# Constants of an attention-and-maxout kernel: two memsets split in halves, a third made a ScalarE copy

## The chip, the cores and the metric

The kernel runs on one core of a Trainium2 chip. A core has five engines that run their own instruction streams and meet at semaphores: TensorE (PE in the profile, its weight loads PEld), VectorE (DVE), ScalarE (ACT), GpSimd (POOL) and SyncE (SP). Data moves between device memory and the on-chip SBUF by DMA queues that SyncE, GpSimd and ScalarE issue; matmul results land in PSUM. The metric is device time in microseconds, the median over runs.

## What is computed

```python
def mab(q, kv):
    s = scale * (q @ kv.transpose(0, 2, 1))
    s = s - s.max(-1, keepdims=True)
    a = np.exp(s)
    a /= a.sum(-1, keepdims=True) + 1e-09
    return a @ kv
h = mab(I, x)                 # 32 inducing points attend to x: (4, 12544, 128)
attn = mab(x, h)              # every row of x attends to the 32 results
g = np.maximum(attn @ w1, attn @ w2)      # (50176, 1024)
out = g @ w_out                           # (50176, 128)
```

The input has four batches of 12,544 rows of 128, the two weight matrices are 128x1024 and the last is 1024x128.

## The kernel before

Everything lies in one function, `tile_isab_inducing__then__act_maxout2_kernel`. The order of the instructions on each engine is written out by hand (`tc.manual_schedule`): a small model of the engines' times, the class `Clock`, decides while the program is built which step comes next, and what results is a fixed list for each engine.

**The head.** SyncE loads the first 14 of 98 chunks of batch 0 as f32 (`xf`, L202) and the inducing points. GpSimd loads the other chunks and casts them to f16 on the way (`load_x`, L165). In between it makes two identity matrices (`make_identity`, which the profile lists under masks.py). After the loads of x come those of the weights (L211 to L213). Meanwhile VectorE sets constants:

- `warm`, 128x512 f16, zero (L214). Operand of nine matmuls (L694) that TensorE runs before any data is there, of fillers later (L794), and of one matmul in each pooling sum.
- `ones16` and `ones32`, 128x128 in f16 and f32, one (L215, L216). A column of `ones16` sums the exponentials of batch 0 (L284) and of the remainder of later batches. `ones32` has no other use.
- `ones_q`, 128x4 f16: zero (L217), then a one in column q for the 32 partitions of quarter q (L219). Operand of the matmul that sums each quarter's exponentials (L670).

Then VectorE and ScalarE cast the first chunks, `xf` to f16 (L690, L691); TensorE transposes them (L233); VectorE and ScalarE copy the results out of PSUM (L244, L247); scores, exponentials (L272) and sums over batch 0 follow, by the list of steps `HEAD`. This part ends at about 24 us.

**The main part.** For each block of 16 chunks (four quarters of up to four chunks, one quarter on 32 partitions each) TensorE makes the scores (L611), ScalarE their exponentials (L630), TensorE four matmuls at a time on its four row groups (`phase`, L1021); VectorE or ScalarE takes the relu of each result (L1037, L1040); TensorE multiplies by `woutp` (L837); VectorE scales the result by the reciprocal of the sum (L864); SyncE stores it. The maximum of w1 and w2 is computed as a relu of the difference plus a linear term. The next batch's pooling (L327, L338, L383) runs in between.

The constants are set in this piece of the head, on VectorE except for the last line:

```python
nc.vector.memset(warm, 0.0)
nc.vector.memset(ones16, 1.0)
nc.vector.memset(ones32, 1.0)
nc.vector.memset(ones_q, 0.0)
for q in range(4):
    nc.vector.memset(ones_q[32 * q : 32 * (q + 1), q : q + 1], 1.0)
nc.gpsimd.memset(m1bd, 0.0)
```

Of the kernel before, what the change touches and what calls it, by code (L numbers as in the profile page):

```python
# [102 lines left out]
def kernel(  # L103
# [9 lines left out]
    nc = tc.nc  # L113
# [64 lines left out]
    ones32 = consts.tile([128, 128], F32, name="ones32")  # L178
    ones16 = consts.tile([128, 128], F16, name="ones16")
    warm = consts.tile([128, 512], F16, name="warm")  # L180
    ones_q = consts.tile([128, 4], F16, name="ones_q")
# [15 lines left out]
    with tc.manual_schedule(engines={ET.PE, ET.DVE, ET.Activation, ET.Pool, ET.SP}):  # L197
# [13 lines left out]
            nc.gpsimd.dma_start(out=w1h[:, lo : lo + 512], in_=moe_w1[:, lo : lo + 512])  # L211
            nc.gpsimd.dma_start(out=w2h[:, lo : lo + 512], in_=moe_w2[:, lo : lo + 512])
        nc.gpsimd.dma_start(out=woutp, in_=moe_w_out.rearrange("(jb j) c -> j jb c", j=128))  # L213
        nc.vector.memset(warm, 0.0)  # L214
        nc.vector.memset(ones16, 1.0)  # L215
        nc.vector.memset(ones32, 1.0)  # L216
        nc.vector.memset(ones_q, 0.0)  # L217
        for q in range(4):
            nc.vector.memset(ones_q[32 * q : 32 * (q + 1), q : q + 1], 1.0)  # L219
        nc.gpsimd.memset(m1bd, 0.0)  # L220
# [1050 lines left out]
```

## Time and profile before

| | |
|---|---|
| median of 3 runs | 327.14 us (327.10 to 327.21) |
| the profiled execution's own time | 327.28 us |
| its span, first to last instruction | 325.4 us |
| TensorE busy | 318.4 us, 98% of the span |
| VectorE busy | 284.3 us, 87% |
| ScalarE busy | 279.7 us, 86% |
| mean granted clock of TensorE | 1.00 |
| TensorE busy in the first 25 us | 21.5 us |
| TensorE busy from 60 to 300 us | 239.6 us of 240 |

The profile is one execution. A line of its timeline gives the start and the duration in microseconds, the engine, the source line, the operation, the tile written and the tile read, and how many instructions are merged in it; in brackets stands how long the engine was idle before, and what ended that. The chain of work that ended last is followed back from the last instruction, at each step to what released it. Starts are counted from the first instruction.

### The profile page before, as it was taken

The page shows a single profiled execution, that of the slowest core. Times are in us where ns is not written, and L with a number is a line of the kernel's source. Part 1 is how long each engine was busy: PE and PEld are TensorE (multiplying, and loading weights), DVE is VectorE, ACT ScalarE, POOL GpSimd, SP SyncE. Part 2 cuts the span into 40 slices and gives each one's busy share as a digit, 9 for nine tenths or more (in the row PEclk, how much of TensorE's full clock was granted, in tenths as well). Part 3 has the DMA queues.
Part 4 walks back from the last instruction along what each step waited for, and adds up shares of the span by engine and source line. Part 5 has one row for each costly group of instructions (what it writes and reads, how often), then busy time and mean ns, then how long its engine had stood idle before and what let it go on. Part 6 is the DMA issues. An engine that isn't in the chain of part 4 may idle for free.

```text
span 325.4 us, 12582 instructions
## 1 busy us (share of the span) xinstructions
PE 318.4 (98%) x5406; PEld 242.4 (74%) x5406; DVE 284.3 (87%) x512; ACT 279.7 (86%) x557; POOL 26.4 (8%) x53
## 2 busy tenths in 40 slices
PE   7899999999999999999999999999999999999996
PEld 3786777777777777777777777777777777777786
DVE  2469989989989998998989999998989999999973
ACT  3559899999888999998988999989969999999961
POOL 7262030000040000000040000000000000000000
PEclk9999999999999999999999999999999999999999
DMA  7999999985189999993479999885312312132133
GB/s 203 208 199 213 275 232 212 194 219 156 76 164 242 227 230 204 178 176 133 130 151 243 208 249 219 175 174 134 116 66 99 115 66 99 74 125 99 68 129 115
DMA packets 71831, 53.65 MB, mean 165 GB/s; under 512 B 52288, under 2 KB 57312, under 8 KB 71776
## 3 DMA queue, kind: packets, MB, share of 16 engines
q1 hardware_dynamic: 65232, 38.57, 49.3%
q0 software_dynamic: 6400, 14.22, 22.6%
q8 instruction: 42, 0.69, 1.0%
q14 instruction: 13, 0.11, 0.1%
q10 hardware_dynamic: 144, 0.07, 0.1%
HBM read 28.33 MB, written 25.69 MB: 166 GB/s over the span
## 4 chain that ended last, share of the span: by engine, by line
PE 93%; DMA 3%; ACT 2%; POOL 1%; issue 0%; DVE 0%; POOLq 0%
PE ps L837 61%; PE ps L1021 22%; DMA xn<-in_x_dram 3%; PE ps L611 2%; PE ps L327 2%; PE ps L383 1%; PE ps L233 1%; PE ps L670 1%; PE ps L301 1%; ACT relu L1037 1%; ACT xT L247 1%; PE ps L256 0%; PE ps L428 0%; PE ps L504 0%; ACT e L630 0%
## 5 line engine op out<-in xcount | busy, mean ns | idle before, releaser
L1037 ACT ACTIVATE relu<-ps 128x512 f16<-128x512 f32 x461 | 244.7, 602 | 27.6 <-PE ps L1021 19.2
L1040 DVE TENSOR_SCALAR relu<-ps 128x512 f16<-128x512 f32 x323 | 206.8, 682 | 16.6 <-PE ps L1021 14.9
L837 PE MATMUL ps<-woutp,relu 128*128 128x128 f16 x3136 | 217.3, 220 | 0.0
L837 PEld LDWEIGHTS <-relu 128*128 128x128 f16 x3136 | 176.7, 98 | 39.6 <-issue 29.3
L1021 PE MATMUL ps<-e,hwd 32*128 32x512 f16 (+2 forms) x888 | 88.7, 358 | 0.3 <-ACT e L630 0.3
L864 DVE TENSOR_TENSOR o<-ps,rp 128x512 f32<-128x512 f32 (+3 forms) x108 | 68.4, 634 | 5.5 <-PE ps L837 3.4
L1021 PEld LDWEIGHTS <-hwd 32*128 32x128 f16 x888 | 24.9, 91 | 21.1 <-issue 1.0
L1021 PE MATMUL ps<-m,e 32*128 32x128 f16 x381 | 38.7, 217 | 0.0
L1021 PEld LDWEIGHTS <-e 32*128 32x128 f16 x381 | 21.2, 92 | 2.6
L165 POOL DMA_DIRECT2D xn<-in_x_dram x31 | 16.8, 554 | 5.6 <-DMA xn<-in_x_dram 2.6
L244 DVE COPY xT<-ps 128x896 f16<-128x896 f16 (+3 forms) x11 | 5.8, 533 | 8.6 <-PE ps L233 8.5
L338 ACT ACTIVATE eu<-ps 128x512 f16<-128x512 f32 x18 | 10.8, 616 | 0.0
L630 ACT ACTIVATE e<-ps 128x512 f16<-128x512 f32 (+2 forms) x21 | 10.5, 577 | 0.0
L164 POOL COPY pace<-hacc 128x1 f32<-128x1 f32 x2 | 0.4, 183 | 114.0 <-DVE hacc L416 114.0
L233 PE MATMUL ps<-identity,xn 128*128 128x128 f16 x98 | 8.1, 229 | 1.4 <-DMA xn<-in_x_dram 1.4
L611 PE MATMUL ps<-xT,hT 128*32 128x512 f16 (+3 forms) x114 | 8.5, 362 | 0.0
L247 ACT COPY xT<-ps 128x896 f16<-128x896 f16 (+3 forms) x8 | 4.9, 640 | 3.9 <-PE ps L233 3.9
L233 PEld LDWEIGHTS <-xn 128*128 128x128 f16 x98 | 6.0, 102 | 2.9 <-DMA xn<-in_x_dram 1.8
L327 PE MATMUL ps<-xT,inducingT 128*32 128x512 f16 x72 | 6.5, 385 | 0.0
L272 ACT ACTIVATE et<-ps 128x224 f16<-128x224 f32 (+3 forms) x11 | 4.1, 410 | 2.5 <-PE ps L256 1.7
L611 PEld LDWEIGHTS <-hT 128*32 128x32 f16 x114 | 3.2, 94 | 3.8 <-issue 2.5
L383 PE MATMUL ps<-xn,eT 128*32 128x128 f16 x288 | 5.5, 220 | 0.0
(92 smaller groups left out, 105.8 us busy)
## 6 DMA issues: line engine op xcount, KB each, us to landing
out_dram<-o SPq DMA_DIRECT2D x85, 256.0 KB, 2.4
xn<-in_x_dram POOLq DMA_DIRECT2D x24, 448.0 KB, 11.3
out_dram<-o SPq DMA_DIRECT2D x20, 128.0 KB, 1.9
xn<-in_x_dram POOLq DMA_DIRECT2D x5, 224.0 KB, 10.8
xn<-in_moe_w_dram POOLq DMA_DIRECT2D x4, 256.0 KB, 14.2
xT<-xn SPq DMA_TRANSPOSE x42, 3.9
xf<-in_x_dram SPq DMA_DIRECT2D x1, 512.0 KB, 3.6
xf<-in_x_dram SPq DMA_DIRECT2D x1, 384.0 KB, 4.1
```

What stands on the lines that cost most here:

```text
L165: nc.gpsimd.dma_start(out=xn_at[b, i][:, 0:n, :], in_=xr[b, :, k0 : k0 + n, :])
L233: nc.tensor.transpose(ps[:, j, :], xn_at[0, i][:, g + j, :], identity16)
L327: nc.tensor.matmul(out=ps[32 * g : 32 * (g + 1), :], lhsT=inducingT, rhs=xT_tiles[b % 2][:, U * u + 4 * g : U * u + 4 * (g + 1), :], start ...
L338: nc.scalar.activation(out=eu, in_=ps, func=AF.Exp, scale=scale, accum_out=st[b]["es"][:, u : u + 1])
L383: nc.tensor.matmul(out=ps[32 * g : 32 * (g + 1), 0:128], lhsT=eT[:, j, 32 * g : 32 * (g + 1)], rhs=xn_of(b, U * v + 4 * g + j), start=(j = ...
L611: nc.tensor.matmul(out=ps[32 * q : 32 * (q + 1), 128 * t : 128 * (t + n)], lhsT=hq, rhs=xT[:, c : c + n, :], start=True, stop=True, tile_p ...
L630: nc.scalar.activation(out=blk.e2[:, lo:hi], in_=ps[:, lo:hi], func=AF.Exp, scale=st[0]["rs"] if blk.b == 0 else scale,)
L837: nc.tensor.matmul(out=g.ps[:, 128 * c : 128 * (c + 1)], lhsT=g.blk.relu[q][:, 128 * (jb * w4 + t) : 128 * (jb * w4 + t + 1)], rhs=woutp[: ...
L864: nc.vector.tensor_mul(osb[:, 0:n, :], g.ps[:, 0 : n * C].rearrange("p (s c) -> p s c", s=n), rp)
L1021: nc.tensor.matmul(**seq[i])
L1037: nc.scalar.activation(out=dst, in_=src, func=AF.Relu)
L1040: nc.vector.tensor_scalar(out=dst, in0=src, scalar1=0.0, scalar2=None, op0=ALU.max)
```

## The change

Six lines replace four in the piece above. `warm` is set in two halves of 256 columns. `ones16` is no longer set by VectorE; ScalarE copies it from `ones32`. `ones_q` is cleared in two halves of 64 partitions. The order on VectorE becomes: warm, warm, ones32, ones_q, ones_q, then the four ones as before. It has one instruction more ahead of the cast of L690, and ScalarE has one more ahead of the cast of L691; its table load now stands before that copy. TensorE's first weight load waits for the first half of `warm`, its first matmul for the second. Nothing else differs in the instruction lists of the five engines but line numbers.

```diff
-        nc.vector.memset(warm, 0.0)
-        nc.vector.memset(ones16, 1.0)
+        nc.vector.memset(warm[:, 0:256], 0.0)
+        nc.vector.memset(warm[:, 256:512], 0.0)
         nc.vector.memset(ones32, 1.0)
-        nc.vector.memset(ones_q, 0.0)
+        nc.scalar.copy(out=ones16, in_=ones32)
+        for h in range(2):
+            nc.vector.memset(ones_q[64 * h : 64 * (h + 1), :], 0.0)
         for q in range(4):
             nc.vector.memset(ones_q[32 * q : 32 * (q + 1), q : q + 1], 1.0)
```

## The prediction

> **What bounds the kernel now.** I read the head of the profile's page first, then its chain of work that ended last, and then the timeline and that chain over the first microseconds, where every changed line lies.
>
> ```profile
> span 325.4 us, 12582 instructions
> PE 318.4 (98%) x5406; PEld 242.4 (74%) x5406; DVE 284.3 (87%) x512; ACT 279.7 (86%) x557; POOL 26.4 (8%) x53
> ...
> PE 93%; DMA 3%; ACT 2%; POOL 1%; issue 0%; DVE 0%; POOLq 0%
> ```
>
> TensorE is busy for 98% of the span and makes up 93% of the chain. VectorE has no share of that chain worth a per cent; DMA and POOL have theirs at the start. The chain over the first four microseconds says what they are:
>
> ```profile
> 1.23 0.04 POOLq masks.py:199
> 1.27 0.63 POOL xn L165
> 1.90 0.18 POOL identity masks.py:197
> ...
> 2.20 0.29 POOL identity masks.py:199
> 2.49 0.50 POOL xn L165
> ...
> 3.52 8.30 DMA xn<-in_x_dram
> ```
>
> (Columns: start, duration, what.) Until 11.82 us the end is set by GpSimd, which issues loads of x between making the identities, and by the transfer issued at 3.52. From there TensorE leads, with short pieces of ScalarE. So a memset on VectorE or a copy on ScalarE in the first two microseconds costs only if it delays GpSimd's issues, the transposes of x, or TensorE's readiness for the chunk that lands at 11.82. The timeline of those microseconds (start, duration, engine, line; in brackets the idle time before, and what ended it):
>
> ```profile
> 0.74 1.28 ACT L691 ACT_TABLE_LOAD   x1 [0.74 <-PEq L1255]
> ...
> 0.86 0.27 DVE L214 MEMSET warm<- 128x256 uint32 x1 [0.86 <-PEq L1255]
> 1.11 0.17 DVE L215 MEMSET ones<- 128x128 f16 x1
> 1.19 0.13 PEld L694 LDWEIGHTS <-warm 128*128 128x128 f16 x2 [1.19 <-DVE warm L214]
> 1.19 4.02 PE L694 MATMUL ps<-warm 128*128 128x512 f16 x9 [1.19 <-DVE warm L214]
> ...
> 1.25 0.17 DVE L216 MEMSET ones<- 128x128 f32 x1
> 1.37 0.06 DVE L217 MEMSET ones_q<- 128x2 uint32 x1
> 1.49 0.35 DVE L219 MEMSET ones_q<- 32x1 f16 x4
> ...
> 4.39 0.73 DVE L690 CAST xn<-xf 128x1024 f16<-128x1024 f32 x1 [2.55 <-DMA xf<-in_x_dram]
> 5.17 0.77 PEld L233 LDWEIGHTS <-xn 128*128 128x128 f16 x8 [0.86 <-DVE xn L690]
> ...
> 5.31 0.83 ACT L691 CAST xn<-xf 128x768 f16<-128x768 f32 x1 [3.29 <-DMA xf<-in_x_dram]
> ```
>
> VectorE is done with its constants at 1.84 and then idle for 2.55 us; ScalarE has loaded its table by 2.02 and is idle for 3.29 us. Both wait for the first rows of x. That is the room in which the change lies.
>
> **The change, part by part.** After the head, every engine's program is the old one, in the old order; VectorE's and ScalarE's come one instruction later in their streams.
>
> *warm in two halves.* One memset of 256 words took 0.272 us. A half is 128 words; the nearest row is the 128-element memset, 0.165 us each (L215, L216), with 0.14 from start to start (1.11 to 1.25). So the second half ends at 0.86 + 0.14 + 0.165 = 1.165 instead of 1.13: 0.03 later. The first weight load now needs only the first half; the first matmul also waits for the second. Queued behind it are the other eight warm matmuls and then the transposes of L233. The warm matmuls come 0.43 apart (their weight loads at 2.02, 2.45, 2.88). The ninth starts at 4.58 and, by that pitch, leaves the array at about 5.01; the transposes wait until 5.17 for the VectorE cast that ends at 5.12. So 0.16 us covers the 0.03. Without this cover it would be 0.03 on the first transposes, which in turn have 0.73 us of TensorE idle behind them (it waits for x at 7.55). Taken: 0; bounds 0 and +0.03.
>
> *ones16 leaves VectorE, ones_q is cleared in two halves.* The memset of ones16 took 0.14 of VectorE's time by pitch (1.11 to 1.25); the second ones_q half adds about 0.10 (the small memsets of L219 come 0.10 apart: 0.35 for four that last 0.06). With +0.03 from warm, the last constant is set at about 1.84 + 0.03 - 0.14 + 0.10 = 1.83. L219's first and third memsets each wait for one half, both cleared before their turn; a repeat of the 0.06 wait seen between L217's end (1.43) and 1.49 would be the most. The cast of L690, next in the queue, waits until 4.39 in any case, and ones_q is first read at 25.4. Taken: 0. If VectorE had no gap there, some 0.06 us.
>
> *ones16 by ScalarE.* Nothing in the trace is a 128x128 copy from f32 to f16 here; the ScalarE copies nearest to it are L462 (128x1, 0.16 us) and L247 (128x256, 0.367 us), so about 0.25. It waits for ones32, ready at 1.14 + 0.165 = 1.31, earlier than the table load that ScalarE needs anyway and that ends at 2.02. It is done by about 2.3, 3.0 us before the cast of L691, which is queued behind it. Readers of ones16 (L284, from 10.11) wait already for ScalarE's exponentials of L272, later in that queue, so they get no new wait. Taken: 0; with no gap, +0.25 on the second half of the first transposes, which have the same 0.73 behind them.
>
> *GpSimd beside it.* No instruction of GpSimd or SyncE changes. But its first issue, 1.23 to 1.90, ran beside VectorE's memsets and took 0.67, the second 0.55 with VectorE idle. If the memsets cause that 0.12, moving them could give it back, or put as much on the memset that follows. These issues lie on the chain above, so the bounds are -0.12 and +0.12; VectorE's busy stretch ends within 0.01 of where it ended, so I take 0.
>
> [...]
>
> Sum: 0, between -0.12 and +0.21 (0.12 + 0.03 + 0.06). The profiled execution took 327.28 us, 1.9 beyond its span and 0.14 above the median of 327.14. On the profile's own time that is 327.28; against the median, with the 0.03 of warm left in as unhidden, 327.2.
>
> **Rivals.**
>
> *The clock of TensorE opens later (slower).* The warm matmuls run at half rate: 0.43 for 512 columns, where the chain's 256-column steps of L474 at 22 us take 0.11 to 0.13. Transposes go from 0.10 apart (eight loads in 0.77 at 5.17) to 0.06 (fourteen in 0.79 at 7.55), so full rate is reached between 5.9 and 7.5, though the granted clock reads 1.00 throughout. If that moment lies on fixed marks and the 0.03 misses one, full rate could come as late as the chunk at 11.87: TensorE is busy 3.78 us in 6.5 to 12.0, half rate adds as much, and the idle 1.72 there absorbs part: 2.1 late at worst, 329.3; the middle is 1.1, 328.2. For it: the start of warm does move. Against: the three runs lie within 0.11 us, and the margin is 0.03 in over 4 us.
>
> [...]
>
> *A page of instructions arrives late (slower).* VectorE's and ScalarE's streams shift by one slot against the blocks in which they are fetched.
>
> ```profile
> q14 instruction: 13, 0.11, 0.1%
> ```
>
> Of the queue table: 13 packets, 0.11 MB, 0.1% of 16 engines' span, so about 0.4 us each. If one became exposed, it would cost that plus the least median from issue to landing in the page, 1.9 us (stores of 128 KB): 2.3, or 329.4, from the point where an engine runs out of fetched instructions. Against it: two such packets pass between 33 and 40 us, and the relu at 37.82 there starts 0.42 after the matmuls that feed it (37.40), just as the one at 151.93 after those at 151.51. Some sixty instructions between the packets leave ample time.
>
> *The shift removes such a stall (faster).* ScalarE's idle 0.56 before 37.82 and 0.73 before 151.93 are put down to TensorE. If they were late instructions instead, the shift could give back one or both: 326.6 to 325.9. The equal lag of 0.42 speaks against it.
>
> **How the numbers follow.** 0.2%, or 0.65 us, is about what can be told from no change. No effect: 0.72, and all of its bounds lie inside 0.2%. Clock later 0.09 and page later 0.08, together slower 0.17. Stall removed: 0.11, faster. The predicted time is 327.2. No effect alone gives 327.0 to 327.5; the range runs from the first faster value, 326.6, to the clock's middle, 328.2, which leaves about 0.15 outside.
>
> **What would show it.** Right: warm's second half ends near 1.17 and the first matmul starts near 1.22; ScalarE's new copy ends before 2.5; the casts still wait for x at 4.4 and 5.3; GpSimd's first issue is still near 0.67, and the transfer issued third still starts near 3.5 and lands near 11.8. Wrong: transposes at 7.55 still 0.10 apart (clock), a relu that starts well over 0.45 after its matmuls on VectorE or ScalarE (pages), or a first wait for x that has moved by more than 0.2.

## The result, and the profile after

| | before | changed |
|---|---|---|
| median, 22 runs each | 327.25 us | 326.62 us |
| ratio | | 0.9984 (95% interval 0.9978 to 0.9991) |
| profiled execution: own time, span | 327.28, 325.4 us | 326.59, 324.8 us |

The change makes the kernel 0.63 us faster by the medians, 0.16% by the ratio. That lies inside the range that was forecast, but the forecast was no effect, and the interval excludes that.

The page after has a span that is 0.6 us shorter; the shares of its chain are the old ones to the per cent and do not say where the time went:

```profile
span 324.8 us, 12584 instructions
...
PE 93%; DMA 3%; ACT 2%; POOL 1%; issue 0%; DVE 0%; POOLq 0%
```

In the head, all steps came out nearly as worked out. The timeline after (the lines behind L217 are shifted by two):

```profile
0.84 0.17 DVE L214 MEMSET warm<- 128x128 uint32 x1 [0.84 <-PEq L1257]
0.98 0.17 DVE L215 MEMSET warm<- 128x128 uint32 x1
1.12 0.17 DVE L216 MEMSET ones<- 128x128 f32 x1
1.20 4.00 PE L696 MATMUL ps<-warm 128*128 128x512 f16 x9 [1.20 <-DVE warm L215]
...
1.23 0.67 POOL L165 DMA_DIRECT2D xn<-in_x_dram  x1 [0.79 <-POOLq L1257]
1.48 0.36 DVE L221 MEMSET ones_q<- 32x1 f16 x4
...
2.03 0.30 ACT L217 CAST ones<-ones 128x128 f16<-128x128 f32 x1
```

The second half of warm ends at 1.15, VectorE's constants at 1.84 as before, ScalarE's copy at 2.33, and GpSimd's first issue takes 0.67 as before. The transfer that leads the chain starts at 3.52 in both and ends at 11.79 instead of 11.82. When the two traces are laid side by side, TensorE instruction by TensorE instruction, it stands within 0.03 us of the old times at 26 us and still at 162 us. The whole gain then comes at two places: 0.35 at 162.40, and 0.22 at 276.93 with another 0.06 at 279.08.

**The first place.** VectorE's timeline around 162 us before, and below it after:

```profile
159.65 1.89 DVE L1040 TENSOR_SCALAR relu<-ps 128x512 f16<-128x512 f32 x3
161.45 0.15 DVE L376 TENSOR_REDUCE hacc<-es 128x1 f32<-128x6 f32 x1
162.05 0.29 DVE L416 TENSOR_TENSOR hacc<-ps,hacc 128x129 f32<-128x129 f32 x1 [0.46 <-PE ps L1021]
```

```profile
159.65 1.89 DVE L1042 TENSOR_SCALAR relu<-ps 128x512 f16<-128x512 f32 x3
161.46 0.15 DVE L378 TENSOR_REDUCE hacc<-es 128x1 f32<-128x6 f32 x1
161.71 0.29 DVE L418 TENSOR_TENSOR hacc<-ps,hacc 128x129 f32<-128x129 f32 x1
```

Up to the reduce the two agree within 0.01 us. Then the addition that completes a batch's pooling starts 0.46 us after the engine is free in the old kernel, and 0.10 after in the new. TensorE needs its result for L428. What TensorE waited for between 30 and 320 us (in total, times, longest) is a single line before, and nothing at all after:

```profile
PE ps L428 <- DVE hacc L416: 0.3, 1, 0.3
```

Could the addition itself have waited for TensorE, as the bracket says? From 159 to 162 us TensorE's matmuls start within 0.01 us of each other in the two profiles, and in the new one the same addition starts 0.34 earlier. So what it needs of TensorE is there by 161.71 in both, and the matmuls in the bracket are not the cause.

**The second place.** ScalarE's timeline from 274 us before, and after:

```profile
274.48 1.09 ACT L1037 ACTIVATE relu<-ps 128x512 f16<-128x512 f32 x2
275.98 1.57 ACT L1037 ACTIVATE relu<-ps 128x512 f16<-128x512 f32 x3 [0.42 <-PE ps L1021]
```

```profile
274.62 2.79 ACT L1039 ACTIVATE relu<-ps 128x512 f16<-128x512 f32 x5
```

The idle time of 0.42 is gone: five relus follow one another. On TensorE the matmuls of L1021 that start next took 0.62 before and 0.40 after. This loss was not in the list of waits above, since it shows there as longer matmuls and not as idle time:

```profile
276.39 0.62 PE L1021 MATMUL ps<-e,hwd 32*128 32x512 f16 x4
```

```profile
276.04 0.40 PE L1023 MATMUL ps<-e,hwd 32*128 32x512 f16 x4
```

**What the two late instructions have in common.** The views of the profile leave out the instructions that only wait for a semaphore. The trace has them. In both places such a wait stands right in front of the late instruction. The wait at 161.64 took 0.02, and the addition began 0.40 after its end; the one at 275.65 took 0.02, and the relu began 0.32 after its end. With the change, both begin 0.04 after it. They are number 319 of VectorE's stream and number 575 of ScalarE's, counted from 0 and with these waits, and the change shifts both streams by one. The packets of the instruction queue q14, 13 of 8,192 bytes each in the span of either profile, move as well. From 275.5 to 278 us the old profile has one and the new has none; from 160 to 162 us it is the other way round. The line of the old one, then that of the new one:

```profile
q14 instruction: 1, 0.01, 1.2%
```

```profile
q14 instruction: 1, 0.01, 1.0%
```

By the trace's own records the two packets in question begin at 162.73 and 276.67 in the old profile, 0.68 and 0.69 after the late instruction has started, and at 161.39 and 274.06 in the new one. So in the old kernel such a packet is not what the late instruction waited for; it may be set off by the same crossing.

### The profile page after: what moved, and what is told of

It reads as the page before. It is cut to its first block, busy times and chain, and to the rows that moved or that the text cites. A ratio compares the mean times of both kernels' runs of the same rounds, so it can differ in the third digit from the quotient of the medians.

```text
span 324.8 us, 12584 instructions
## 1 busy us (share of the span) xinstructions
PE 317.5 (98%) x5406; PEld 241.9 (74%) x5406; DVE 284.3 (88%) x513; ACT 280.1 (86%) x558; POOL 26.4 (8%) x53
## 4 chain that ended last, share of the span: by engine, by line
PE 93%; DMA 3%; ACT 2%; POOL 1%; issue 0%; DVE 0%; POOLq 0%
PE ps L839 61%; PE ps L1023 22%; DMA xn<-in_x_dram 3%; PE ps L613 2%; PE ps L329 2%; PE ps L385 1%; PE ps L235 1%; PE ps L672 1%; PE ps L303 1%; ACT relu L1039 1%; ACT xT L249 1%; PE ps L258 0%; PE ps L506 0%; ACT e L632 0%; PE ps L796 0%
```

## The experiments

The theory to be tested, called the page theory in the expectations, is this: instructions reach an engine in blocks; the first instruction of a block comes some 0.3 us late; and this shows when a wait stands right in front of it, since the engine then has nothing queued. The rival, called the head theory: the constants, now set at another moment and partly by ScalarE, set the engines going differently. All kernels start from the kernel before. What they add or cut writes `ones32` only, which nothing there uses. The ratios below are not the quotients of the medians beside them and differ from those by up to 0.0007; the intervals belong to the ratios.

### Each engine alone

```diff
-        nc.vector.memset(ones32, 1.0)
+        nc.vector.memset(ones32[:, 0:64], 1.0)
+        nc.vector.memset(ones32[:, 64:128], 1.0)
```

> Kernel before, with the memset of the unused ones32 split in two: VectorE's stream one slot later, ScalarE's as before, all constants set in the old order. Page theory (an instruction that follows a wait of the sequencer and is the first of a block of 128 instructions starts about 0.3 us late): VectorE's addition at L416 starts 0.06 us instead of 0.42 after the reduce before it, the wait of TensorE at L428 (162.4) is gone, and the ScalarE relu that starts at 275.98 stays 0.28 late; time 0.34 below before, ratio 0.9989 to 0.9990. Head theory (the time comes from constants set at another moment in the first 2 us): nothing changes at 162, and the time is within 0.1 us of before.

```diff
         nc.vector.memset(ones32, 1.0)
+        nc.scalar.copy(out=ones32[:, 1:2], in_=ones32[:, 0:1])
```

> Kernel before, with one ScalarE copy of a 128x1 column of the unused ones32 in the head: ScalarE's stream one slot later, VectorE's as before. Page theory: the wait at L428 at 162.4 stays, the relu at 275.98 starts 0.28 earlier against its neighbours, and TensorE gains some 0.29 from 276 on; time 0.29 below before, ratio 0.9991. Head theory: if the gain came from ScalarE working before the first cast, all of the 0.6 us or none, and not from 276 on alone.

Measured: with VectorE's stream shifted alone 327.02 us, ratio 0.9986 (0.9975 to 0.9998); with ScalarE's alone 327.15, ratio 0.9993 (0.9983 to 1.0002); before, on the same chip, 327.43. In the first, TensorE gains 0.35 at 162.4 and nothing at 276; in the second it gains nothing at 162.4 and 0.28 from 276 on. The wait of L428 is gone from the first profile and stands in the second. Its line there, with the line number shifted by one:

```profile
PE ps L429 <- DVE hacc L417: 0.3, 1, 0.3
```

So the gain splits into two parts, one for each engine, and each part comes and goes with that engine's own shift. The second interval reaches just past 1; what decides there is the place in the trace.

### The same shift with an untouched head

```diff
             step += 1
+            if step == 500:
+                nc.vector.memset(ones32[:, 0:1], 1.0)
+                nc.scalar.copy(out=ones32[:, 1:2], in_=ones32[:, 2:3])
```

> Kernel before with an untouched head; at about 71 to 75 us VectorE gets a 128x1 memset and ScalarE a 128x1 copy, both on the unused ones32. They cost some 0.06 and 0.16 us of two engines that TensorE does not wait for there. Page theory: both late starts (162.05 and 275.98) go, as with the change: 0.63 below before, ratio 0.998, or up to 0.2 less if the two small instructions reach TensorE. Head theory: no gain, 0 to 0.2 slower.

The other kernel has step 2900 in place of 500:

> The same two small instructions, put at about 282 to 285 us, behind both late starts. Page theory: both stay, time within 0.1 of before (0 to 0.2 slower if the small instructions reach TensorE). A theory by which any added instruction or any new phase between the engines helps would give about as much as the run with them at 71 to 75 us.

Measured: 326.74 us, ratio 0.9972 (0.9961 to 0.9982), with the two instructions at 73.29 and 75.05 us; 327.44, ratio 0.9998 (0.9990 to 1.0007), with them behind both places. In the first profile TensorE gains 0.35 at L428 and 0.28 from the second place on, as with the change. Two small instructions that do nothing useful give the whole gain of the change if they stand ahead of the two places, and none if they stand behind. The edit of the head is not needed for the gain. The late kernel's VectorE timeline still has the gap:

```profile
161.73 0.15 DVE L376 TENSOR_REDUCE hacc<-es 128x1 f32<-128x6 f32 x1
162.34 0.29 DVE L416 TENSOR_TENSOR hacc<-ps,hacc 128x129 f32<-128x129 f32 x1 [0.46 <-PE ps L1021]
```

### Other shifts

VectorE one slot earlier: the memset of `ones32` is left out.

> Kernel before without the memset of ones32, which nothing reads: VectorE's stream one slot earlier, ScalarE's as before. Page theory: the block now begins with the relu behind the addition at L416. The addition starts 0.06 after the reduce as in the changed kernel, the relu behind it some 0.1 later than there because its fetch is half hidden by the addition, and TensorE's wait at L428 goes; ScalarE's relu at 275.98 stays late. 0.34 below before, ratio 0.9990. A theory by which a later stream (one more instruction) is what helps expects no gain or a loss here.

VectorE five slots later: the memset of `ones32` is cut in six.

> Kernel before with the memset of ones32 cut in six: VectorE's stream five slots later, ScalarE's as before. Page theory: the block now begins with the relu that starts at 159.65 in the old profile, which also follows a wait of the sequencer. That relu starts some 0.35 later than before against its neighbours, the four VectorE instructions behind it are pushed by as much, so that the addition at L416 and TensorE's L428 come as late as in the kernel before (162.05 and 162.40): no gain, ratio 0.9995 to 1.0005. A theory by which the place of the addition alone matters expects the 0.34 to be gained here too.

Measured: 327.00 us, ratio 0.9998 (0.9989 to 1.0006), and 327.41, ratio 1.0008 (0.9997 to 1.0018); before 327.22. By the times alone both are no change, and the first expectation of 0.9990 is neither borne out nor excluded. The traces decide. In the first, TensorE gains 0.35 at L428, and the relu behind the addition is the one that comes late. In the second, the late instruction is the relu at 159.65. VectorE's timeline there:

```profile
158.94 0.68 DVE L869 TENSOR_TENSOR o<-ps,rp 128x512 f32<-128x512 f32 x1
160.06 1.89 DVE L1045 TENSOR_SCALAR relu<-ps 128x512 f16<-128x512 f32 x3 [0.44 <-PE ps L1026]
161.87 0.15 DVE L381 TENSOR_REDUCE hacc<-es 128x1 f32<-128x6 f32 x1
162.12 0.29 DVE L421 TENSOR_TENSOR hacc<-ps,hacc 128x129 f32<-128x129 f32 x1
```

The idle time of 0.44 now stands in front of the relus, the addition follows the reduce at once, and still it starts at 162.12, as late as before. The chain of work that ended last has the stall of this kernel under its right name, "issue", time in which the engine waited for nothing that the profile shows:

```profile
159.69 0.38 issue
160.06 0.70 DVE relu L1045
```

From the trace, the starts of four VectorE instructions in us from an earlier wait that all five kernels share, by the shift of VectorE's stream:

```
number in the kernel before      0 (before)  +1 (change)  +1 alone   -1      +5
314  relu at 159.65                1.366       1.367        1.367    1.367   1.714
318  the wait                      3.358       3.358        3.356    3.356   3.704
319  addition, L416                3.774       3.423        3.422    3.422   3.769
320  the relu behind it            3.983       3.675        3.675    3.817   3.979
```

Late is number 319 with no shift, 320 with -1, and 314 with +5. In the shifted stream each of these is number 319. So what is late belongs to the place in the stream and not to the instruction that stands there. How much of it shows depends on what stands in front. Behind a wait it is 0.35 us (shift 0 and +5). With -1 the instruction in front is the addition and not a wait, and 0.14 shows. With +1 the place falls on the wait itself, which waits for the reduce in front of it in any case, and nothing shows.

### Both streams by other amounts

Both streams two slots later:

> Kernel before with the memset of ones32 cut in three and two ScalarE copies of a column of it in the head: both streams two slots later. Page theory: both blocks begin with instructions that follow no wait, so both late starts are gone; but on ScalarE the block before now begins with the relu at 211.35, which follows a wait at 211.22 and would start about 0.2 late. 0.63 below before if TensorE does not need that relu, 0.4 if it does: ratio 0.9981 to 0.9988.

VectorE one slot earlier, ScalarE one slot later:

> Kernel before without the memset of ones32 and with one 128x1 ScalarE copy of a column of ones16 in the head: VectorE's stream one slot earlier, ScalarE's one later. Page theory: both late starts go as in the changed kernel, by opposite shifts: 0.63 below before, ratio 0.998, the same as the changed kernel. A theory by which both streams have to be later expects half of it, 0.29.

Measured: 326.60 us, ratio 0.9978 (0.9966 to 0.9990), and 326.71, ratio 0.9981 (0.9971 to 0.9992). Two slots later on both engines, or one earlier on VectorE and one later on ScalarE, give what the change gives: in both profiles TensorE gains 0.35 at L428 and 0.28 from the second place on. The direction does not matter; the amount can, as the five slots above show. One detail of the first expectation was a miss: the ScalarE relu at 211.35 did not start late. A wait behind it came 0.12 later, without effect on TensorE, and it does so in every kernel with ScalarE shifted by one or two. Which of ScalarE's instructions is first in that block is therefore not settled.

None of these is faster than the changed kernel by more than the intervals allow.

## Why the prediction was wrong

- **What bounds the kernel, and the parts of the change: right.** The sum of 0 for the head held: 0.03 at most at 26 us. warm, ones_q, the copy (0.30 us instead of the 0.25 estimated) and GpSimd's issue came out as worked out or within 0.05. The 0.12 that GpSimd's first issue takes longer than the second stayed with other memsets beside it.
- **The step that failed.** The sum has no term for the shift of the two streams by one slot. The rival that would have given one, "The shift removes such a stall", was set aside because "the equal lag of 0.42 speaks against it". The lag was that of two relus whose idle times, 0.56 and 0.73, really were waits for TensorE; they are unchanged after. That said nothing of the rest of the streams. The two stalls that existed, at 162.05 on VectorE and 275.98 on ScalarE, were not looked at; the shift removed both, 0.35 and 0.28 of TensorE's time. The first was in plain sight in the old profile: 0.46 idle in front of L416 is put down to matmuls of L1021, but L428's line is the only wait of TensorE that the view lists in 290 us. The second shows only as ScalarE's idle 0.42.
- **The other rival's ground was too simple as well.** "Some sixty instructions between the packets leave ample time" would make every crossing free. If the two late places are crossings, these cost 0.28 and 0.35, where the engine had nothing in front of them but a wait. The count of sixty was the author's estimate: in the old trace VectorE starts 125 instructions and ScalarE 127, waits included, from the packet at 36.56 us to the one at 97.56.
- **The price** put on a removed stall was 0.56 to 0.73 each. Measured: 0.35 on VectorE and on TensorE for the first, 0.28 on ScalarE and on TensorE for the second, 0.63 together. That the result of 326.62 meets this rival's 326.6 is luck: that figure was the price of one stall of 0.56, at a place that was no stall, and the range reached down to it for this reason alone.
- **The clock rival** did not decide: the changed kernel's profile has full clock, and its fourteen transposes at 7.58 take 0.96 as before. The moment of full rate did move, to the early side: the weight loads of the first eight transposes, at 5.17 in both, took 0.54 instead of 0.77. Those behind them waited for x, so nothing was gained by it.

Shown by runs: that the gain sits in these two places, that each belongs to one engine's stream, and, for VectorE, that the late place is fixed in the stream. On ScalarE the four kernels with one slot more ahead of the place and the one with two lose the late start, and none moves it onto another instruction. Inferred only: that the fixed place is the first instruction of a fetched block. For it: 319 and 575 lie 256 apart, and of the old profile's 13 packets ten can each be put beside a number 63, 191, 319, 447 or 575 of one of the two streams, at most 2.4 us from its start. Not settled: at the other eight of these numbers nothing visible is late, and no run shows what the late instruction waits for.

## What to carry to other kernels

An instruction added to a stream shifts all that follows in it, by the page theory against the blocks in which it is fetched. In this kernel a place of the stream that is late anyway cost 0.28 or 0.35 us where it fell right behind a semaphore wait and TensorE needed the result soon, and one harmless instruction more ahead of it, on VectorE also one less, took this away. In a kernel bound by one engine, list that engine's waits over the steady part first: a lone wait for an engine whose inputs were ready is worth a look at the trace's own records. A gain of this kind says nothing of the edit that caused it, and the next edit can undo it.

## What the runs showed of the hardware that was not expected

TensorE's clock can be withdrawn in the head for one execution and not for another of the same kernel. In the profiled execution of the kernel with ScalarE shifted alone the granted clock (the column in front of the last two) falls to half between 8 and 9 us:

```profile
7.00:8.00 1.00, 0.17 (x3) 0.18 (x4) 0.00 (x0) 0.98 (x1) 0.09 (x1) 1.00 1.03 204
8.00:9.00 1.00, 1.00 (x15) 0.81 (x12) 0.57 (x1) 0.04 (x1) 0.53 (x1) 0.67 1.07 215
9.00:10.00 1.00, 0.72 (x18) 0.68 (x18) 0.67 (x4) 0.90 (x1) 0.00 (x0) 0.50 1.07 212
```

That execution took 328.49 us, 1.3 above its kernel's median; the kernel's eleven others read a mean granted clock of 0.999 or 1.000. In it TensorE is 1.6 us behind the old profile at 15 us. The profiled execution of the kernel with two instructions at 71 to 75 us, whose head is the old one, has the same: granted clock 0.86 from 6 to 8 us and 0.50 from 8 to 14, 328.27 us against a median of 326.74. Executions above 328.3 occur in the kernel before too, 5 of 35 beside the last four experiments, four of them at a mean granted clock of 0.990 to 0.995 and one at 1.000. This is the cost that the clock rival priced at 1.1 to 2.1, here 1.3 and 1.5 above the medians, but it comes by execution and not by edit. What withdraws the clock is not shown by any run here.
